# Second image's statistics by TensorE ones products, and a transposed embedding product, in a fused residual block

## The chip, the cores and the metric

The kernel runs on one core of one Trainium2 chip. The metric is the device time of one execution in microseconds (us); the runs of the kernel before gave 490.58, 489.97 and 493.06, a median of 490.58. Engines are named as in the profile: PE (TensorE matmul), PEld (its weight loads), DVE (VectorE), ACT (ScalarE), POOL (GpSimd), SP (SyncE, which issues most DMAs).

## The reference

```python
B, C, HW, E = 2, 512, 64, 1152
def reference(x, t_emb, g1, be1, w1, w_emb, g2, be2, w2):
    # gn: normalisation over 4 groups of 128 channels x 64 x 64; conv3: 3x3 convolution, 512 to 512 channels
    h = conv3(_silu(gn(x, g1, be1)), w1)
    emb = _silu(t_emb) @ w_emb
    h = h + emb.reshape(B, C, 1, 1)
    h = conv3(_silu(gn(h, g2, be2)), w2)
    return x + h
```

All inputs and the output are bfloat16. A group of the normalisation is exactly one tile of 128 channels, so its statistics are one mean and one variance per image and tile.

## The kernel before, in words

**Tiling.** The channels are four tiles (ct) of 128. The work is cut into eight chunks: layer 1 or 2, image 0 or 1, upper or lower half of the rows; chunks 0 and 1 are image 0 in layer 1, chunks 2 and 3 image 1 in layer 1, 4 to 7 the same in layer 2. A chunk has four units, one for each tile k of output channels. The convolution is a Winograd-like transform along the rows: the input side makes planes of the normalised rows (`rows_a`, `rows_b`: L614 to L663), PE multiplies them with transformed weights, ACT evacuates the PSUM banks with a scale (`evac_*`, L737 to L753), and DVE combines the results (L826 to L841).

**A unit** (`unit`, L713) in chunk 0 is a list of steps of 12 matmuls of 512 columns (4 tiles ct x 3 column taps): p2, p0, p1, p3 into rotating pairs of banks 0 to 5, p4 into bank 6 and p5 into bank 7. For the first three units p4 and p5 are made in the opening (L1091 to L1095), into banks 0 to 5, so banks 6 and 7 are first used for convolution in unit 3 of chunk 0. Chunks 1 to 3 have in place of p2 and p0 the steps B2, B0, A2, A0 of 256-column matmuls, with p4 in bank 6 ahead of B and p5 in bank 7 behind B.

**Statistics of image 1** (`stats1`, L1023). They are needed by the silu of chunk 2. `CFG["st1"]` (L205) says how each tile is summed. With 1 (tiles 0, 2, 3) ACT reads six pieces of 650 or 715 elements twice, once as Identity and once as Square, each with an accumulator output (L1031, L1032), and DVE adds the six partial sums (L1034 to L1038). With 0 (tile 1) DVE makes `bn_stats` of eight pieces (L1048) and `bn_aggr` (L1050). Tile k is registered behind unit k of chunk 0 (L1129). Then `gn_chain` (L429), put on the list `later` by tile 3 (L1056), sums over the 128 channels of a tile with `ones_neg` products into bank 7, copies the bank with DVE (L442) and makes scale and offset. It is registered behind the first unit of chunk 1.

**Embedding** (`emb`, L1058). Registered in chunk 0 ahead of unit 1. Three pieces of `w_emb` go through one buffer. Per piece three matmuls have `s_sb` (128 x 2, silu of `t_emb`) as weights and 512 columns of `w_emb` as moving data, into two partitions of bank 7. DVE copies them (L1071), and four fp32 transposes bring the 512 sums onto the 128 partitions, as `EMB`.

**Order of the work.** Each operation is registered with a planner (`Plan`, L26): engine, cost, read and written regions, from which follow its predecessors in the order of registration. Convolution steps are chained in the order of registration; other PE operations float. `solve` (L143) simulates the engines as in-order queues with these costs and `emit` (L164) writes the instructions in the order of the start times found. So who stands behind whom on an engine comes from the planner, while two operations on one PSUM bank keep their order of registration. All DMAs of the parts spoken of here are issued by SP, in that order.

Of the kernel before, what the change touches and what calls it, by code (L numbers as in the profile page):

```python
# [10 lines left out]
ACT = mybir.ActivationFunctionType  # L11
# [165 lines left out]
def _idx(off, dims):  # L177
# [7 lines left out]
RW = 65  # L185
# [19 lines left out]
    'st1': (1, 0, 1, 1),  # L205
# [9 lines left out]
def kernel(  # L215
# [807 lines left out]
    def stats1(ct):  # L1023
        nm = f"st1{ct}"
        me, mq = ME1 + ct, ME1 + CT + ct
        if CFG["st1"][ct]:
            part = Fc(12)
            for i, (ch, r0, n) in enumerate([(ch, r0, n) for ch in range(2) for r0, n in ((1, 11), (12, 11), (23, 10))]):
                d = A(VB[0] + (2 * (ct % 2) + i % 2) * VP + 3120, [[1, n * RW]], BF16)
                dma(d.ap, x[1, ct, ch][:, r0 * RW:(r0 + n) * RW], [], [d], P * n * RW * 2, nm)  # L1030
                act(A8(JNK, n * RW), d, ACT.Identity, acc=F(part + i), name=nm)  # L1031
                act(A8(JNK, n * RW), d, ACT.Square, scale=float(HW) ** -0.5, acc=F(part + 6 + i), name=nm)  # L1032
            wj = Fc(6)
            pl.op("DVE", 0.1, lambda: nc.vector.tensor_scalar(  # L1034
                out=F(wj, 6).ap, in0=F(part, 6).ap, scalar1=1.0 / HW, scalar2=0.0, op0=ALU.mult, op1=ALU.add,
                accum_out=F(me).ap), regs(F(part, 6)), regs(F(wj, 6), F(me)), nm)
            pl.op("DVE", 0.1, lambda: nc.vector.reduce_sum(out=F(mq).ap, in_=F(part + 6, 6).ap, axis=AX.X),  # L1037
                  regs(F(part + 6, 6)), regs(F(mq)), nm)  # L1038
        else:
            bst, mv = Fc(48), Fc(2)  # L1040
            for i in range(4):
                d = A(W2O[0], [[1, 16 * RW]], BF16)
                r0 = 1 + 16 * (i % 2)
                dma(d.ap, x[1, ct, i // 2][:, r0 * RW:(r0 + 16) * RW], [], [d], P * 32 * RW, nm)
                for h in range(2):
                    e = A(W2O[0] + h * 8 * RW, [[RW, 8], [33, 2], [1, 32]], BF16)
                    q = F(bst + 12 * i + 6 * h, 6)
                    pl.op("DVE", 0.61, lambda e=e, q=q: nc.vector.bn_stats(out=q.ap, in_=e.ap), regs(e), regs(q), nm)  # L1048
# [8 lines left out]

    def emb():  # L1058
        nm = "emb"
        pe = R(psum[0:BB, 7 * 512:8 * 512], ("P", np.array([7])), 512)  # L1060
        lst = []
        lds = []
        for i0, n in ((0, 3), (3, 3), (6, 3)):
# [142 lines left out]
```

## Time and profile before

| | |
|---|---|
| median of 3 runs | 490.58 us |
| the profiled execution: time, span | 490.7 us, 488.9 us |
| PE busy | 460.8 us (94%), 2853 matmuls |
| PE weight loads | 279.1 us (57%) |
| DVE busy | 435.8 us (89%) |
| ACT busy | 379.8 us (78%) |
| POOL busy | 37.4 us (8%) |
| DMA | 87.17 MB, mean 178 GB/s |

The profile is of one execution. In the waits view a row says which engine's line waited for which engine's line, the sum in us, how often and the longest. In the timeline a row is a run of equal instructions: start, duration, engine, line, operation, output and input with sizes, count, and in brackets the idle time ahead of it and what ended it. In the windows view a row is a stretch: its length, the busy time and count of PE, PEld, DVE, ACT and POOL, the clock granted to PE, and the DMA share with GB/s. A group row gives the total busy time and the mean duration in ns, then idle time ahead. L380 is the helper that issues all matmuls, L329 DVE's two-operand operations, L352 all ACT operations, L365 the DMAs. The ends of matmuls are modelled; their starts are not.

### The profile page before, as it was taken

The page shows a single profiled execution, that of the slowest core. Times are in us where ns is not written, and L with a number is a line of the kernel's source. Part 1 is how long each engine was busy: PE and PEld are TensorE (multiplying, and loading weights), DVE is VectorE, ACT ScalarE, POOL GpSimd, SP SyncE. Part 2 cuts the span into 40 slices and gives each one's busy share as a digit, 9 for nine tenths or more (in the row PEclk, how much of TensorE's full clock was granted, in tenths as well). Part 3 has the DMA queues.
Part 4 walks back from the last instruction along what each step waited for, and adds up shares of the span by engine and source line. Part 5 has one row for each costly group of instructions (what it writes and reads, how often), then busy time and mean ns, then how long its engine had stood idle before and what let it go on. Part 6 is the DMA issues. An engine that isn't in the chain of part 4 may idle for free. (4 is left out here: it accounts for less than half of the span.)

```text
span 488.9 us, 8107 instructions
## 1 busy us (share of the span) xinstructions
PE 460.8 (94%) x2853; PEld 279.1 (57%) x2853; DVE 435.8 (89%) x865; ACT 379.8 (78%) x612; POOL 37.4 (8%) x66
## 2 busy tenths in 40 slices
PE   6999999777499999999999998999999999999995
PEld 5744344343255555555555555666666667676783
DVE  1699999997869999998899999998799999998547
ACT  4887899999699987859997886865977579656552
POOL 3100000000100001010000000112111021001000
PEclk9999999989599999999999999999999999999999
DMA  8754463464832336657477776685956769737524
GB/s 329 296 168 116 154 182 117 155 200 135 287 105 108 114 114 181 177 152 278 137 280 266 278 260 211 146 211 135 242 149 183 196 175 248 172 82 139 122 45 87
DMA packets 41080, 87.17 MB, mean 178 GB/s; under 512 B 6480, under 2 KB 16720, under 8 KB 41040
## 3 DMA queue, kind: packets, MB, share of 16 engines
q1 hardware_dynamic: 36096, 77.60, 47.7%
q0 software_dynamic: 4656, 9.05, 12.4%
q8 instruction: 22, 0.36, 0.3%
q14 instruction: 18, 0.15, 0.1%
q10 hardware_dynamic: 288, 0.01, 0.0%
HBM read 62.25 MB, written 31.32 MB: 191 GB/s over the span
## 5 line engine op out<-in xcount | busy, mean ns | idle before, releaser
L380 PE MATMUL psum<-ar 128*128 128x256 f16 (+2 forms) x2737 | 445.5, 325 | 11.7 <-DVE ar L329 5.7
L329 DVE TENSOR_TENSOR ar<-ar 128x1040 f16<-128x1040 f16 (+6 forms) x689 | 405.8, 647 | 31.4 <-ACT ar L352 26.9
L380 PEld LDWEIGHTS <-ar 128*128 128x128 f16 (+1 forms) x2729 | 266.5, 99 | 187.6 <-issue 17.3
L352 ACT ACTIVATE ar<-ar 128x384 bf16<-128x384 bf16 (+6 forms) x205 | 169.1, 856 | 50.9 <-DVE ar L329 45.7
L352 ACT ACTIVATE ar<-psum 128x512 f16<-128x512 f32 (+2 forms) x220 | 152.5, 718 | 40.7 <-PE psum L380 31.3
L352 ACT ACTIVATE ar<-ar,fs 128x2112 f16<-128x2112 bf16 (+1 forms) x32 | 68.6, 2148 | 5.9 <-DMA ar<-h_scr 3.3
L333 DVE TENSOR_SCALAR ar<-ar 128x512 f16<-128x512 f16 (+2 forms) x73 | 26.2, 380 | 2.0 <-ACT ar L352 2.0
L365 POOL DMA_DIRECT2D out_dram<-ar x15 | 18.1, 1206 | 108.9 <-DVE ar L329 108.9
L352 ACT ACTIVATION_READ_ACCUMULATOR ar<-psum 128x1 f32 x96 | 19.7, 205 | 0.0
L451 POOL TENSOR_TENSOR fs<-fs 128x1 f32<-128x1 f32 (+1 forms) x7 | 7.6, 1083 | 137.4 <-DVE fs L449 137.4
L369 POOL MEMSET ar<- 128x65 f16 (+5 forms) x28 | 4.4, 197 | 123.6 <-DVE ar L329 47.2
L380 PE MATMUL psum<-ar,ones_bf 128*128 128x260 bf16 x64 | 9.6, 308 | 4.4 <-DMA ar<-in_x_dram 4.4
L380 PE MATMUL psum<-fs,ones_neg 128*128 128x1 f32 (+3 forms) x36 | 5.2, 258 | 7.0 <-DVE fs L1037 7.0
L352 ACT ACTIVATION_READ_ACCUMULATOR ar<-ar 128x1 f32 x56 | 11.1, 198 | 0.0
L380 PEld LDWEIGHTS <-ones_bf 128*128 128x128 bf16 x64 | 6.7, 108 | 6.2 <-issue 3.1
L380 PEld LDWEIGHTS psum<-fs,ones_neg 128*128 128x128 f32 x36 | 5.0, 206 | 8.1 <-DVE fs L1037 7.2
L365 POOL DMA_DIRECT2D ar<-ar x4 | 3.7, 931 | 71.3 <-DVE ar L329 60.5
L968 DVE SCALAR_TENSOR_TENSOR ar<-psum,ident 128x128 bf16<-128x128 f32 x4 | 1.2, 289 | 5.6 <-PE psum L380 5.6
L1048 DVE BATCH_NORM_STATS2 fs<-ar 128x6 f32<-128x512 bf16 x8 | 5.3, 680 | 0.0
L442 DVE COPY fs<-psum 128x2 f32<-128x2 f32 (+1 forms) x7 | 1.1, 159 | 4.4 <-PE psum L380 4.4
L453 DVE TENSOR_TENSOR fs<-fs 128x1 f32<-128x1 f32 (+1 forms) x7 | 1.1, 155 | 1.9 <-POOL fs L451 1.9
L411 ACT ACT_TABLE_LOAD x1 | 1.3, 1283 | 1.7 <-PEq L1190 1.7
(50 smaller groups left out, 23.1 us busy)
## 6 DMA issues: line engine op xcount, KB each, us to landing
ar<-in_w_dram SPq DMA_DIRECT2D x32, 384.0 KB, 4.0
ar<-in_x_dram SPq DMA_DIRECT2D x16, 552.5 KB, 4.0
h_scr<-ar SPq DMA_DIRECT2D x16, 520.0 KB, 3.1
ar<-h_scr SPq DMA_DIRECT2D x16, 520.0 KB, 3.5
out_dram<-in_x_dram SPq DMA_DIRECT2D x30, 260.0 KB, 4.2
out_dram<-ar POOLq DMA_DIRECT2D x15, 520.0 KB, 6.1
u_scr<-ar SPq DMA_DIRECT2D x16, 384.0 KB, 3.1
ar<-u_scr SPq DMA_DIRECT2D x4, 1536.0 KB, 7.4
```

The source lines that it names most:

```text
L329: pl.op("DVE", 0.075 + 0.000521 * out.n, lambda: nc.vector.tensor_tensor(out=out.ap, in0=a.ap, in1=b.ap, op=op), regs(a, b), regs(out), name)
L333: pl.op("DVE", cost or 0.075 + 0.00026 * out.n, lambda: nc.vector.tensor_scalar(out=out.ap, in0=a.ap, scalar1=s, scalar2=None, op0=ALU.mul ...
L352: lambda: nc.scalar.activation(out=out.ap, in_=a.ap, func=func, scale=sc, **kw), regs(*rr), regs(*ww), name)
L365: lambda: eng.dma_start(out=out, in_=in_, **kw), regs(*r), regs(*w), name, lat=3.2 if sw else None, after=after, sw=sw)
L369: pl.op("POOL" if eng == "gpsimd" else "DVE", 0.08 + 0.0005 * out.n, lambda: e.memset(out.ap, v), (), regs(out), name)
L380: nc.tensor.matmul(out.ap, lhsT=lhsT.ap, rhs=rhs.ap, start=st, stop=sp, skip_group_check=True)
L411: nc.scalar.activation(out=fs[:, WARM:WARM + 1], in_=fs[:, WARM + 1:WARM + 2], func=ACT.Silu)
L442: pl.op("DVE", 0.16, lambda: V.tensor_copy(out=F(tot, 2 * n).ap, in_=ps.ap), regs(ps), regs(F(tot, 2 * n)), name)
L451: pl.op("POOL", 0.85, lambda: nc.gpsimd.tensor_tensor(out=F(rs, n).ap, in0=N.ap, in1=F(NEGH, n).ap, op=ALU.pow), regs(N), regs(F(rs, n)), ...
L453: small(lambda: V.tensor_mul(out=S.ap, in0=F(rs, n).ap, in1=F(g, n).ap), [F(rs, n)], [S], name)
L968: pl.op("DVE", 0.3, lambda: nc.vector.scalar_tensor_tensor(out=j2.ap, in0=g.ap, scalar=1.0 / HW, in1=ident[:], op0=ALU.mult, op1=ALU.mult, ...
L1048: pl.op("DVE", 0.61, lambda e=e, q=q: nc.vector.bn_stats(out=q.ap, in_=e.ap), regs(e), regs(q), nm)
```

## The change

`stats1` has one form for all four tiles. A tile comes in four pieces of 1040 elements, in three slots that rotate (the free tails of three planes of chunk 0). Over each piece PE runs four products of 260 columns with a matrix of ones as weights (`cone`), all sixteen of a tile accumulated in bank 6 or 7 by turns; ACT squares the piece once, with an accumulator; at the end ACT sums the 260 columns of the bank with one Identity with accumulator. DVE adds four partial sums of squares. Identity passes over the data, `bn_stats` and the table `st1` are gone. The four tiles are registered ahead of chunk 0's units, and `gn_chain` right behind unit 3 of chunk 0, where it was behind the first unit of chunk 1. `emb` is registered ahead of these, with five loads of `w_emb` into places that are free in the opening, and 36 products with blocks of `w_emb` (128 x 128) as weights and `s_sb` (2 columns) as moving data; the sums land on the 128 partitions as `EMB` needs them, with no copy and no transposes.

```diff
-    'st1': (1, 0, 1, 1),
...
     def stats1(ct):
         nm = f"st1{ct}"
         me, mq = ME1 + ct, ME1 + CT + ct
-        if CFG["st1"][ct]:
-            part = Fc(12)
-            for i, (ch, r0, n) in enumerate([(ch, r0, n) for ch in range(2) for r0, n in ((1, 11), (12, 11), (23, 10))]):
-                d = A(VB[0] + (2 * (ct % 2) + i % 2) * VP + 3120, [[1, n * RW]], BF16)
-                dma(d.ap, x[1, ct, ch][:, r0 * RW:(r0 + n) * RW], [], [d], P * n * RW * 2, nm)
-                act(A8(JNK, n * RW), d, ACT.Identity, acc=F(part + i), name=nm)
-                act(A8(JNK, n * RW), d, ACT.Square, scale=float(HW) ** -0.5, acc=F(part + 6 + i), name=nm)
...
+        bk = 6 + ct % 2
+        part = Fc(4)
+        for i in range(4):
+            pb = VB[0] + (ct * 4 + i) % 3 * VP + 3120
+            d = A(pb, [[1, 1040]], BF16)
+            r0 = 1 + 16 * (i % 2)
+            dma(d.ap, x[1, ct, i // 2][:, r0 * RW:(r0 + 16) * RW], [], [d], P * 2080, nm)
+            mm([(Ps(bk, 0, [[1, 260]]), cone, A(pb + 260 * q, [[1, 260]], BF16),
+                 i == 0 and q == 0, i == 3 and q == 3) for q in range(4)], nm, chain=False)
+            act(A8(VB[0] + 3 * VP + 3120 + i % 2 * 520, 1040), d, ACT.Square, scale=float(HW) ** -0.5, acc=F(part + i), name=nm)
+        act(A(VB[0] + 3 * VP + 3120, [[1, 260]], BF16), Ps(bk, 0, [[1, 260]]), ACT.Identity, scale=1.0 / (P * HW), acc=F(me), name=nm)
+        pl.op("DVE", 0.1, lambda: nc.vector.reduce_sum(out=F(mq).ap, in_=F(part, 4).ap, axis=AX.X),
+              regs(F(part, 4)), regs(F(mq)), nm)
...
     def emb():
         nm = "emb"
-        pe = R(psum[0:BB, 7 * 512:8 * 512], ("P", np.array([7])), 512)
...
+        at = [VB[0] + i // 2 * VP + 3120 + i % 2 * 512 for i in range(8)] + [JNK]
+        for i in range(0, ET, 2):
+            n = min(2, ET - i)
+            d = A(at[i], [[1, n * 512]], BF16)
+            dma(d.ap, w_emb[:, i:i + n, :].rearrange("p e o -> p (e o)"), [], [d], P * n * 1024, nm)
+        lst = [(Ps(7, k * BB, [[1, BB]]), A(at[i] + k * 128, [[1, 128]], BF16), R(s_sb[:, i, :], K("s_sb"), 2),
+                i == 0 and k == 0, i == ET - 1 and k == CT - 1) for i in range(ET) for k in range(CT)]
         mm(lst, nm, chain=False)
...
     ucnt[0] = 0
+    emb()
+    for ct in range(CT):
+        stats1(ct)
...
-                if k == 1:
-                    emb()
...
             run_later = list(later)
-            later.clear()
+            if c == 0 and k < CT - 1:
+                run_later = []
+            for f in run_later:
+                later.remove(f)
             unit(c, k, opening=2 if c == 0 and k < 3 else 0)
             for f in run_later:
                 f()
-            if c == 0:
-                stats1(k)
```

The planner then finds another order on every engine. Three places follow; line numbers of the change are one less than those of before from L206 on.

On PE, before, the products of image 1's `gn_chain` (the two rows with `ones_neg`) stand between the last B step (128x256) and step p5 (128x8x2x32 and 128x512) of the second unit of chunk 1:

```order
L380 LDWEIGHTS ar
L380 MATMUL psum<-ar 128x256
L380 MATMUL psum<-fs,ones_neg 128x8 [waits DVE_49]
L380 MATMUL psum<-fs,ones_neg 128x4
L380 LDWEIGHTS ar
L380 MATMUL psum<-ar 128x8x2x32 [waits DVE_49]
```

In the change they stand inside the B steps of the first unit of chunk 1:

```order
L379 LDWEIGHTS ar
L379 MATMUL psum<-ar 128x256
L379 MATMUL psum<-fs,ones_neg 128x8 [waits Activation_49]
L379 MATMUL psum<-fs,ones_neg 128x4
L379 LDWEIGHTS ar
L379 MATMUL psum<-ar 128x256
```

So they moved ahead by about one unit of 80 matmuls, and what follows them directly is no longer a step that uses their bank.

On ACT, before, from unit 3 of chunk 0 on (128x512 from psum are evacuations, 128x8x2x32 those of p4 and then p5, 128x715 and 128x650 the pieces of image 1's tile 2, 128x384 the first weights of layer 2):

```order
L352 ACTIVATE ar,fs<-psum 128x512 [waits PE_49]
L352 ACTIVATE ar,fs<-ar 128x715 [waits Activation_49]
L352 ACTIVATE ar,fs<-psum 128x8x2x32 [waits DVE_49]
L352 ACTIVATE ar,fs<-ar 128x650 [waits DMAHW2_49,Activation_49]
L352 ACTIVATE ar<-ar 128x512 [waits DVE_49]
...
L352 ACTIVATE ar,fs<-ar 128x715 [waits Activation_49]
L352 ACTIVATE ar,fs<-psum 128x8x2x32 [waits DVE_49]
L352 ACTIVATE ar,fs<-ar 128x715 [waits DMAHW5_49,Activation_49]
L352 ACTIVATE ar<-ar 128x384 [waits DMAHW4_49]
```

In the change, from the last pieces of tile 3 (128x1040) on, with the last evacuation of the sums (128x260):

```order
L351 ACTIVATE ar,fs<-psum 128x8x2x32 [waits PE_49]
L351 ACTIVATE ar,fs<-ar 128x1040 [waits DMAHW3_49,Activation_49]
L351 ACTIVATE ar<-ar 128x512
L351 ACTIVATE ar,fs<-psum 128x512 x2
L351 ACTIVATE ar,fs<-ar 128x2080 [waits Pool_49]
L351 ACTIVATE ar,fs<-psum 128x260 [waits PE_49,Activation_49]
L351 ACTIVATE ar<-ar 128x384 [waits DMAHW4_49]
L351 ACTIVATE ar<-ar 128x384 [waits DMAHW5_49]
L351 ACTIVATE ar<-ar 128x512 [waits DVE_49]
L351 ACTIVATE ar,fs<-psum 128x8x2x32 [waits PE_49]
```

All pieces of image 1 now stand ahead of the evacuation of p5 of unit 3; before, those of tile 3 and a third of those of tile 2 stood behind it. The 128x2080 is the square of a unit's result, which now stands between the last piece and the last sum.

On PE in the change, the last groups of ones products stand inside step p0 of unit 3, each group behind its load (DMAHW):

```order
L379 LDWEIGHTS ones_bf
L379 MATMUL psum<-ar,ones_bf 128x260 [waits DMAHW2_49]
L379 LDWEIGHTS ones_bf
...
L379 MATMUL psum<-ar,ones_bf 128x260 [waits DMAHW3_49]
...
L379 LDWEIGHTS ar [waits DVE_49]
...
L379 MATMUL psum<-ar 128x8x2x32 [waits Activation_49]
```

The last row is the first matmul of p5 of unit 3, six matmuls of p0 behind the last group. Before, no ones products stood in the units. The 36 products of the embedding stand in the opening, among its p4 and p5 products; before, three groups of three stood in units 0 to 2, and the transposes behind them.

38 lines of the change are left out of this document (removed).

## The prediction

> **What bounds the kernel now.** First I read the slices of the page, then the waits of the two stretches in which TensorE (PE) is not full, then the timeline there.
>
> ```profile
> PE   6999999777499999999999998999999999999995
> PEclk9999999989599999999999999999999999999999
> ```
>
> A slice is 12.2 us. PE is full but for the opening, slices 7 to 10 (86 to 134 us) and the tail, and the granted clock drops in slices 8 and 10. From 134 us to 473 us PE's work is an all but unbroken stream, so a microsecond taken out ahead of it moves the end by about one, as long as VectorE (DVE) and ScalarE (ACT) can follow. The waits of 80 to 110 us and of 110 to 145 us, the rows of PE:
>
> ```profile
> PE psum L380 <- DVE ar L329: 3.8, 2, 3.5
> PE psum L380 <- ACT ar L352: 2.2, 1, 2.2
> ...
> PE psum L380 <- DVE fs L1037: 7.0, 1, 7.0
> PE psum L380 <- DVE fs L442: 2.2, 1, 2.2
> ```
>
> The four long ones sum to 2.2 + 3.5 + 7.0 + 2.2 = 14.9 us. What is behind the 7.0 and the second 2.2 stands in the timeline:
>
> ```profile
> 123.19 0.20 ACT L352 ACTIVATION_READ_ACCUMULATOR ar<-ar 128x1 f32 x1
> ...
> 125.97 0.15 DVE L1037 TENSOR_REDUCE fs<-fs 128x1 f32<-128x6 f32 x1
> ...
> 126.19 1.01 PE L380 MATMUL psum<-fs,ones_neg 128*128 128x8 f32 x4 [6.95 <-DVE fs L1037]
> ...
> 129.41 15.76 PE L380 MATMUL psum<-ar 128*128 128x512 f16 x80 [2.21 <-DVE fs L442]
> ```
>
> The `ones_neg` products are those of the second image's `gn_chain`. They use PSUM bank 7, and so does step p5 of unit 1 of chunk 1 behind them; in PE's queue nothing passes them. So PE stands until the last squares of that image have left ACT (123.4), DVE has summed them (126.1) and copied the bank (129.4). ACT is late because it is full:
>
> ```profile
> 60.00:80.00 20.00, 20.00 (x94) 8.95 (x93) 19.22 (x39) 19.50 (x47) 0.00 (x0) 1.00 0.55 159
> 101.70:105.10 3.40, 3.40 (x18) 2.24 (x16) 3.40 (x9) 2.75 (x9) 0.00 (x0) 0.50 0.72 258
> 129.40:132.40 3.00, 2.99 (x8) 1.05 (x8) 2.88 (x8) 0.52 (x1) 0.93 (x1) 0.50 0.81 262
> ```
>
> Columns: stretch, length, busy PE, weight loads, DVE, ACT, POOL, granted clock, DMA. From 60 to 80 us ACT is busy 19.5 of 20. After each of the two groups of waits PE works at half clock, for 3.4 us and for 3.0 us.
>
> **The change, part by part.** The sum is made against the profiled execution's 490.7 us (span 488.9, 1.8 around it); the runs' median is 490.58, the same within 0.1, so nothing is converted.
>
> *ACT and DVE.* The rows of the three tiles that went through ACT and the one that went through DVE:
>
> ```profile
> L352 ACT ACTIVATE ar<-ar 128x715 fp8e4<-128x715 bf16 x24 | 19.1, 797 | 0.2 <-DMA ar<-in_x_dram 0.2
> L352 ACT ACTIVATE ar<-ar 128x650 fp8e4<-128x650 bf16 x12 | 8.9, 745 | 0.3 <-DMA ar<-in_x_dram 0.3
> L1048 DVE BATCH_NORM_STATS2 fs<-ar 128x6 f32<-128x512 bf16 x8 | 5.3, 680 | 0.0
> ```
>
> The accumulator read that follows each overlaps it in part, so the pair takes from ACT what lies between its start and that of the next instruction:
>
> ```profile
> 87.21 1.94 ACT L352 ACTIVATE ar<-ar 128x2080 fp8e4<-128x2080 f16 x1 [0.19 <-DVE ar L329]
> ...
> 89.14 0.58 ACT L352 ACTIVATE ar<-psum 128x512 f16<-128x512 f32 x1
> ...
> 89.71 0.79 ACT L352 ACTIVATE ar<-ar 128x715 fp8e4<-128x715 bf16 x1
> ...
> 90.49 0.58 ACT L352 ACTIVATE ar<-psum 128x512 f16<-128x512 f32 x1
> ```
>
> 0.78 us for 715 elements, 1.93 for 2080. Out go 24 x 0.78 + 12 x about 0.73 = 27.5 us. In come 16 squares of 1040 (between the two rows, 1.05 each: 16.8) and four evacuations of 260 columns (from 0.58 for 512, at most 0.5 each: 2.0), 18.8. ACT saves 8.7 us before the sums are needed. DVE loses 5.3 us of statistics, the embedding's 512-wide copy and some ten operations on a few columns, by estimate 6.5 in all. Both lie beside PE, so neither is a term. They decide whether the waits go. Where the sums are done and needed in the new order, on the clock of before:
>
> ```profile
> 99.60 0.59 ACT L352 ACTIVATE ar<-psum 128x512 f16<-128x512 f32 x1
> ...
> 100.82 18.41 PE L380 MATMUL psum<-ar 128*128 128x512 f16 x99 [3.46 <-DVE ar L329]
> ```
>
> The first row is the evacuation of p5 of unit 3; in the order of the change the last evacuation of the sums stands on ACT ahead of it, so 24 us ahead of 123.4. The second row is PE in p4 of the first unit of chunk 1; the `gn_chain` products now stand among the B steps right behind it, later than the sums. I take all four waits as gone: **-14.9**. Two of them (3.5 and the first 2.2) are of other work: chunk 1's planes from DVE, and the evacuation of bank 6 by ACT behind the squares. With DVE 6.5 and ACT 8.7 us lighter and PE arriving later, both should be on time. If these two stay, 5.7 less is saved. PE's ends are modelled, with a mean of 388 ns for a matmul that follows its predecessor by about 223:
>
> ```profile
> L380 PE MATMUL psum<-ar 128*128 128x512 f16 x1248 | 290.3, 388 | 11.1 <-DVE ar L329 5.3 <-DVE fs L442 3.4 <-ACT ar L352 2.2
> ```
>
> so each wait hides up to 0.17 more; three of the four follow such a matmul: **-0.5**. The half clock goes with the waits: (3.4 + 3.0) / 2 = **-3.2** (0 if waits over some 3 us remain).
>
> *The ones products.* 64 of 260 columns, each with its weight load, enter PE's stream where it is full. The opening of before has the same instruction in a stream:
>
> ```profile
> 18.46 1.98 PE L380 MATMUL psum<-ar,ones_bf 128*128 128x260 bf16 x16
> 20.27 1.24 PE L380 MATMUL psum<-ar 128*128 128x128 bf16 x17
> 21.44 0.83 PE L380 MATMUL psum<-fs,ones_neg 128*128 128x2 f32 x6
> ```
>
> Sixteen from 18.46 to 20.27 are 0.113 each: **+7.2**. Nothing hides them. The rows of the weight loads, of 128 columns, of the ones and of the embedding's 2 columns:
>
> ```profile
> L380 PEld LDWEIGHTS <-ar 128*128 128x128 f16 x1888 | 184.9, 98 | 87.9 <-issue 2.4 <-DVE ar L329 0.8
> L380 PEld LDWEIGHTS <-ones_bf 128*128 128x128 bf16 x64 | 6.7, 108 | 6.2 <-issue 3.1 <-DVE ones_bf L386 1.2
> L380 PEld LDWEIGHTS <-s_sb 128*2 128x2 bf16 x9 | 0.5, 82 | 1.7 <-issue 1.3
> ```
>
> With loads of 108 ns that no longer overlap it would be 14: the upper bound. Below 7 there is no reason to go.
>
> *The embedding product.* Out of the units go nine products, three at a time, and the transposes behind them:
>
> ```profile
> 51.49 0.81 PE L380 MATMUL psum<-ar,s_sb 128*2 128x512 bf16 x3
> 52.24 6.85 PE L380 MATMUL psum<-ar 128*128 128x512 f16 x30
> ...
> L380 PE MATMUL psum<-ar 2*128 2x2 f32 x8 | 1.0, 249 | 0.0
> ```
>
> 3 x 0.75 + at most 1.0 = -3.2. Into the opening come 36 pairs of a 128-column load and a 2-column product. The nearest row is the 17 products of 128 columns above, from 20.27 to 21.44: 0.069 a pair, +2.5; 0.1 a pair (a bare load) would make 3.6. They stand among the opening products, where PE waits a little anyway:
>
> ```profile
> 32.45 19.11 PE L380 MATMUL psum<-ar 128*128 128x512 f16 x84 [0.67 <-DVE ar L329]
> ```
>
> That covers 0.7 of it. Net -3.2 + 2.5 - 0.7 = **-1.4** (0 to -2). [...] The five loads of `w_emb` are queued on SyncE behind most of the first weights, ahead of the last four 192 KB weight loads; the DMA engines have room for them in the ten us behind:
>
> ```profile
> 20.00:30.00 10.00, 10.00 (x70) 6.24 (x69) 8.44 (x25) 9.08 (x13) 1.74 (x2) 1.00 0.15 56
> ```
>
> The share of 0.15 (56 GB/s) leaves the 1.2 MB time before PE is at the last two channel tiles. If those weights came late, the opening products of these tiles would wait.
>
> *What is late next.* The new sums sit in banks 6 and 7. Unit 3's p4 and p5 use those banks, so p5 must wait for the evacuation of the last sum. Six matmuls (1.3 us) lie between the last ones product and p5; the evacuation takes 0.6 and may stand behind a 2080-wide square of 1.93. That is 0 to 3.0 (square, evacuation, and a product late by a landing); I take 1.93 + 0.6 - 1.3 = **+1.2**. Behind p5 in PE's queue stand p1 and p3 of the unit, and ACT's evacuations wait for them.
>
> Sum: -14.9 - 0.5 - 3.2 + 7.2 - 1.4 + 1.2 = -11.6, **479.1 us**.
>
> **The rivals.**
>
> *DVE becomes the bound.* For: it is nearly full behind the stall, and PE would run 12 us ahead of where DVE stood.
>
> ```profile
> 102.00:112.00 10.00, 10.00 (x55) 5.85 (x54) 8.93 (x27) 9.35 (x24) 0.00 (x0) 0.84 0.63 213
> 112.00:122.00 10.00, 7.23 (x41) 3.80 (x39) 7.68 (x16) 9.21 (x24) 0.00 (x0) 1.00 0.45 120
> ...
> 132.00:142.00 10.00, 10.00 (x54) 5.18 (x53) 4.61 (x10) 8.29 (x11) 0.73 (x1) 0.98 0.39 135
> ...
> 160.00:170.00 10.00, 10.00 (x55) 5.19 (x53) 9.90 (x21) 9.94 (x17) 0.00 (x0) 1.00 0.28 87
> ```
>
> Against: in the first three rows it idles 1.1 + 2.3 + 5.4 = 8.8 us, because the second image's planes could not be made without its sums; that idle time and the 6.5 of removed work make 15.3, more than PE's 11.6. If it cannot use the idle time, the end moves by the 6.5 alone: 484.2.
>
> *The banks and loads take back a part.* p4 and p5 of unit 3 wait the full 3.0 each, and the 3.5 for chunk 1's planes stays: -11.6 + 4.8 + 3.5 = -3.3, 487.4. For: ACT and DVE are full up to there. Against: both have less to do.
>
> *Slower: PE stands for its loads.* Each ones group is in PE's queue and waits for its piece; each piece needs one of three slots, which is free again only when PE and ACT have both read it, and its load is issued by SyncE in order, behind loads that wait for other buffers.
>
> ```profile
> ar<-in_x_dram SPq DMA_DIRECT2D x4, 260.0 KB, 2.8
> ...
> DMA to landing us min/median/max: 2.3/3.9/8.2
> ```
>
> A turn of a slot is a landing, the wait in ACT's queue (some 2 us, an estimate) and the square: 2.8 + 2 + 1.05 = 5.9 us; 16 pieces over 3 slots are 5.3 turns, 31 us. From the first unit to p5 of unit 3, where all sums must be done, PE has 180 matmuls of 0.223 and the products: 40 + 7 = 47 us. So loads would have to be slow: with landings of 8.2 and 3 us in ACT's queue a turn is 12.3 and all are 65. PE stands 18 us, the 11.6 are gained, and half clock comes back for some 4 us (+2): 490.7 - 11.6 + 18 + 2 = 499. The point from which the kernel is slower is a turn of 10.7 us. [...] Against this rival: 179 KB pieces made ACT wait 0.5 us in all before, and the embedding's loads, in the same queue, made PE wait for nothing.
>
> *It does not do what it says:* the sums come no sooner, because a load or SyncE holds them. Then the 7.2 of products fall into PE's standing time ahead of the `gn_chain` products, and what is left is the embedding's -1.4: 489.3. Against it is the order: the last evacuation stands 24 us ahead.
>
> **How the numbers follow.** Forecast 0.68 (own range 476 to 483.5), DVE bound 0.12, banks and loads 0.09, slower 0.07, no effect 0.04. The range: below, the forecast without its 1.2 and without the waits of the 512-column row above that lie behind the four (5.3 - 3.8 and 3.4 - 2.2, 2.7 in all), 475.2, rounded to 475.5; above, the DVE rival with 2 us more, 486.0; about 0.18 lies outside. A measurement of this kernel can tell 1% (4.9 us) from no change. Faster by over 1% (under 485.7): 0.68 and most of the DVE rival, 0.80. Within 1%: the bank rival, the rival without effect and the rest, 0.13. Slower: 0.07.
>
> **What would show it.** Right: no PE wait over 2 us between 40 and 140 us; the `ones_neg` products of the second image before 110 us; 64 ones products among units 0 to 3 at 0.11 us each; ACT under 95% from 60 to 80 us; DVE at most 3 us idle from 100 to 140; the clock at 1.00 in the slices 8 to 10. Wrong: waits of PE for `in_x_dram` in the units (the slower rival), DVE rows ahead of PE's waits from 140 us on (the DVE rival), or PE waiting on ACT before p4 or p5 of unit 3 for over 3 us.

## The result and the profile after

The change takes **476.49 us** (476.18 to 478.71), before took 490.28 beside it: a ratio of 0.9716, 95% interval 0.9670 to 0.9762, so 2.8% faster. The profiled execution took 476.65 us with a span of 474.9 (before 490.7 and 488.9): 14.05 less, where 11.6 were predicted.

The slices of the page, PE's busy tenths and the clock:

```profile
PE   6998999899999999999999999999999999999995
PEclk9998999999999999999999999999999999999999
```

The hole in slices 7 to 10 is filled but for one wait (the 8 of slice 7), and the clock is full there; one slice of the opening (35.6 to 47.5 us) has a lower clock, which no term of the prediction had. The waits view from 80 to 145 us, PE's rows, where before had 14.9 us in four, and from 145 to 400 us:

```profile
PE psum L379 <- ACT ar L351: 1.7, 1, 1.7
```

```profile
PE psum L379 <- DVE fs L441: 1.2, 2, 0.9
```

For the second stretch before had three rows:

```profile
PE psum L380 <- DVE ar L329: 1.3, 2, 0.9
PE psum L380 <- DVE fs L442: 1.2, 1, 1.2
PE psum L380 <- ACT ar L352: 0.3, 1, 0.3
```

What is left of PE's waits between 80 and 145 us is one, in PE's timeline at the end of p0 of unit 3 of chunk 0:

```profile
87.75 1.06 PE L379 MATMUL psum<-ar,ones_bf 128*128 128x260 bf16 x8
88.65 1.50 PE L379 MATMUL psum<-ar 128*128 128x512 f16 x6
91.86 0.83 PE L379 MATMUL psum<-ar 128*128 128x512 f16 x3 [1.72 <-ACT ar L351]
```

and on ACT at the same time:

```profile
89.40 1.95 ACT L351 ACTIVATE ar<-ar 128x2080 fp8e4<-128x2080 f16 x1
91.23 0.21 ACT L351 ACTIVATION_READ_ACCUMULATOR ar<-ar 128x1 f32 x1
91.32 0.40 ACT L351 ACTIVATE ar<-psum 128x260 bf16<-128x260 f32 x1
```

The last ones products end at 88.65, the six products of p0 fill PE until about 90.1, and p5 stands until ACT has done the 2080-wide square and then the evacuation of the last sum. Behind it the `gn_chain` products of image 1 now cost nothing:

```profile
99.65 4.37 PE L379 MATMUL psum<-ar 128*128 128x512 f16 x25
103.85 0.51 PE L379 MATMUL psum<-fs,ones_neg 128*128 128x8 f32 x4
104.22 28.05 PE L379 MATMUL psum<-ar 128*128 128x256 f16 x154
```

The ones products of the units (shortest, median and longest record in ns, first and last start in us) and the group row of the squares:

```profile
L379 PE MATMUL psum<-ar,ones_bf x64: 271/275/278, 50.1 to 88.5; 128*128 128x260 bf16 x64
```

```profile
L351 ACT ACTIVATE ar<-ar 128x1040 fp8e4<-128x1040 bf16 x16 | 17.0, 1062 | 0.6 <-ACT ar L351 0.2 <-DVE ar L328 0.2
```

Where in the program the time came from is seen by counting the products of each engine's order along the trace. Start of a step's first product, us, in the profiled executions of before, of the change, and of the change run a second time (further down):

| step | before | change | change again |
|---|---|---|---|
| unit 0 of chunk 0 | 40.7 | 42.8 | 42.0 |
| unit 3, p4 | 76.4 | 80.6 | 79.9 |
| unit 3, p5 | 84.9 | 91.9 | 91.4 |
| chunk 1, unit 0 | 95.2 | 99.9 | 99.4 |
| chunk 1, unit 1 | 114.7 | 114.6 | 113.9 |
| chunk 1, unit 2 | 140.6 | 128.8 | 128.1 |
| chunk 3, unit 0 | 227.1 | 215.2 | 214.9 |
| chunk 7, unit 0 | 434.4 | 420.7 | 420.4 |

Up to unit 0 of chunk 1 the change is 4.7 us behind; two units later it is 11.8 ahead, and 2 more come in small pieces later. The change again has the same order of instructions on every engine.

### The profile page after: what moved, and what is told of

Its sections match the earlier page's. It is cut to its first block, busy times and chain, and to the rows that moved or that the text cites. A ratio compares the mean times of both kernels' runs of the same rounds, so it can differ in the third digit from the quotient of the medians.

```text
span 474.9 us, 8229 instructions
## 1 busy us (share of the span) xinstructions
PE 461.3 (97%) x2936; PEld 283.4 (60%) x2936; DVE 428.2 (90%) x847; ACT 371.9 (78%) x580; POOL 38.8 (8%) x66
## 4 chain that ended last, share of the span: by engine, by line
PE 40%; DVE 24%; ACT 7%; issue 4%; POOL 0%; DVEq 0%; ACTq 0%; POOLq 0%
PE psum L379 40%; DVE ar L328 22%; ACT ar L351 7%; DVE ar L332 2%; POOL fs L450 0%; POOL ar L364 0%; DVEq L1176 0%; DVE fs L441 0%; DVE fs L914 0%; DVE fs L915 0%; DVE fs L452 0%; DVE fs L917 0%; DVE fs L921 0%; DVEq L328 0%; ACTq L351 0%
## 5 line engine op out<-in xcount | busy, mean ns | idle before, releaser
L379 PE MATMUL psum<-ar 128*128 128x512 f16 (+2 forms) x2729 | 443.7, 325 | 4.3 <-ACT ar L351 1.7
L328 DVE TENSOR_TENSOR ar<-ar 128x1024 f16<-128x1024 f16 (+5 forms) x689 | 404.0, 648 | 27.4 <-ACT ar L351 24.2
L351 ACT ACTIVATE ar<-psum 128x512 f16<-128x512 f32 (+2 forms) x224 | 156.5, 714 | 53.3 <-PE psum L379 44.7
L351 ACT ACTIVATE ar<-ar 128x512 f16<-128x512 f16 (+6 forms) x185 | 158.1, 890 | 31.2 <-DVE ar L328 30.2
L364 POOL DMA_DIRECT2D out_dram<-ar x15 | 18.1, 1207 | 115.9 <-DVE ar L328 91.8
L379 PE MATMUL psum<-ar,ones_bf 128*128 128x260 bf16 x128 | 18.3, 284 | 4.5 <-DMA ar<-in_x_dram 4.5
L351 ACT ACTIVATION_READ_ACCUMULATOR ar<-psum 128x1 f32 x100 | 20.8, 208 | 0.0
L379 PEld LDWEIGHTS <-ones_bf 128*128 128x128 bf16 x128 | 12.6, 100 | 9.9 <-issue 3.2
L450 POOL TENSOR_TENSOR fs<-fs 128x1 f32<-128x1 f32 (+1 forms) x7 | 9.0, 1281 | 108.9 <-DVE fs L448 97.2
L351 ACT ACTIVATION_READ_ACCUMULATOR ar<-ar 128x1 f32 x36 | 7.1, 198 | 0.0
```

Of the source, the lines that this page charges most:

```text
L328: pl.op("DVE", 0.075 + 0.000521 * out.n, lambda: nc.vector.tensor_tensor(out=out.ap, in0=a.ap, in1=b.ap, op=op), regs(a, b), regs(out), name)
L351: lambda: nc.scalar.activation(out=out.ap, in_=a.ap, func=func, scale=sc, **kw), regs(*rr), regs(*ww), name)
L364: lambda: eng.dma_start(out=out, in_=in_, **kw), regs(*r), regs(*w), name, lat=3.2 if sw else None, after=after, sw=sw)
L379: nc.tensor.matmul(out.ap, lhsT=lhsT.ap, rhs=rhs.ap, start=st, stop=sp, skip_group_check=True)
L450: pl.op("POOL", 0.85, lambda: nc.gpsimd.tensor_tensor(out=F(rs, n).ap, in0=N.ap, in1=F(NEGH, n).ap, op=ALU.pow), regs(N), regs(F(rs, n)), ...
```

## The experiments

The times are medians of four to ten executions; before stood at 490.2 to 490.5 beside each group. The expectations of some runs count the images from one: their "image 2" is the second image, image 1 of the text above.

**1. The order alone.** Before, with `gn_chain` registered behind unit 1 of chunk 1.

```diff
-            later.clear()
+            if c == 1 and k == 0:
+                run_later = []
+            for f in run_later:
+                later.remove(f)
```

> The kernel before, with one edit: the second image's gn_chain is registered behind unit 1 of chunk 1 instead of behind unit 0, so that p5 of unit 1 no longer stands behind it in bank 7. The sums are still made by ACT and DVE as before. Theory (late sums): the 7.0 and 2.2 us waits on PE go from that place, but chunk 2's planes cannot be made without the sums, which still come at about 123 us, so DVE stands and PE waits at the first unit of chunk 2 or at p4 and p5 of unit 2 for some 6 to 9 us: 484 to 489 us. Rival (order alone): the whole loss came from where the products stood in the queue; 490.3 - 9.2 - 1.5 = 480 or less, with no new wait.

485.81 us, ratio 0.9904 (0.9876 to 0.9931). It leaves out one dependency: tile 0 of chunk 2 is registered ahead of `gn_chain`, so its silu does not wait for the statistics and works with a scale and offset that are not made yet. Chunk 1 gains all that the change gains (its unit 2 starts at 126.1, before at 140.6), and then, as the theory said, PE stands at the first unit of chunk 2 for DVE's planes:

```profile
152.79 3.50 PE L380 MATMUL psum<-ar 128*128 128x512 f16 x15
156.79 0.83 PE L380 MATMUL psum<-ar 128*128 128x512 f16 x3 [0.49 <-DVE ar L329]
166.55 3.78 PE L380 MATMUL psum<-ar 128*128 128x512 f16 x14 [8.94 <-DVE ar L329]
```

**2. The order alone, with the dependency.** Tile 0 of chunk 2 is registered behind `gn_chain` as well.

```diff
...
+            if c == 1 and k == 1:
+                prod(2, 0)
-            if c + 1 < 8:
+            if c + 1 < 8 and not (c == 1 and k == 0):
                 prod(c + 1, k)
```

> The kernel before, with image 2's statistics chain asked for behind unit 1 of chunk 1 and the first tile of image 2's chunk asked for behind it in turn, so that nothing stands ahead of what it needs. Theory (the place of the chain alone cannot bring the gain, since sums that end late push the first tile of image 2 late): waits at chunk 1 shrink as in the earlier run of this kind, and a wait for VectorE of 7 to 12 us stands at the first unit of chunk 2; 484 to 491. Rival (order alone is the gain): 480 or less.

492.67 us, ratio 1.0036 (1.0016 to 1.0055), 1.7 above the theory's range and far from the rival's. PE, at the same place:

```profile
157.63 2.83 PE L380 MATMUL psum<-ar 128*128 128x512 f16 x12
165.01 1.44 PE L380 MATMUL psum<-ar 128*128 128x512 f16 x3 [4.55 <-DVE ar L329]
173.46 2.93 PE L380 MATMUL psum<-ar 128*128 128x512 f16 x10 [7.00 <-DVE ar L329]
```

Unit 2 of chunk 1 starts at 130.3, 10 us ahead of before; unit 1 of chunk 2 at 187.0, 3 behind it. The stall is only pushed from the users of bank 7 to the users of the statistics. For the 7.0 and the second 2.2 us of before the late sums were the cause, not the place of the chain.

**3. The change without ones products.** The sums by Identity passes on ACT over the same 1040-wide pieces, whose four results DVE adds; all else as in the change.

```diff
...
-            mm([(Ps(bk, 0, [[1, 260]]), cone, A(pb + 260 * q, [[1, 260]], BF16),
-                 i == 0 and q == 0, i == 3 and q == 3) for q in range(4)], nm, chain=False)
+            act(A8(VB[0] + 3 * VP + 3120 + i % 2 * 520, 1040), d, ACT.Identity, scale=1.0 / HW, acc=F(part + 4 + i), name=nm)
...
```

> The change without the ones products: each piece of 1040 elements is read twice by ACT, as Identity and as Square, each with accumulator; pieces, slots and the place of registration are those of the change. PE has 7.2 us less, ACT some 15 us more than in the change. Theory (ACT was the late engine): ACT is full again ahead of chunk 1, PE waits for evacuations in units 2 and 3 and for the first planes of chunk 2: 478 to 484 us, with PE waits on ACT of 6 us or more between 60 and 170 us. Rival (larger pieces and the earlier registration were enough, the products only cost): 476.5 - 7.2 - 1.7 = 468 to 471 us.

485.04 us, ratio 0.9894 (0.9862 to 0.9926), 1.0 above the theory's range; the profiled execution took 482.04. PE is rid of 7.2 us of products, and waits instead, for ACT in unit 3 and at the start of chunk 1 (98.53):

```profile
81.63 3.06 PE L379 MATMUL psum<-ar 128*128 128x512 f16 x13
88.97 4.46 PE L379 MATMUL psum<-ar 128*128 128x512 f16 x12 [4.28 <-ACT ar L351]
94.65 2.83 PE L379 MATMUL psum<-ar 128*128 128x512 f16 x12 [1.21 <-ACT ar L351]
98.53 1.72 PE L379 MATMUL psum<-ar 128*128 128x512 f16 x7 [1.06 <-ACT ar L351]
```

and 3.4 us for DVE at the first unit of chunk 2. So of the 13.8 us, the ones products bring 8.6 by the medians (485.04 - 476.49 = 8.55) and 5.4 between the profiled executions (482.04 - 476.65): 7.2 us on the fullest engine are the cheaper price. The profiled execution lies 3.0 us under the median of its run, and its mean granted clock is 0.995 where the other three have 0.985 to 0.988; so up to 3 of the 8.6 us may be clock that this trace does not show.

**4. The embedding alone.** Before, with the change's embedding in the opening and nothing else.

```diff
...
+    emb()
     for c in range(8):
...
-                if k == 1:
-                    emb()
```

> The kernel before, with the transposed embedding product in the opening alone; the second image's sums as before. Theory: the 7.0 us wait of PE on the last sums stays, as ACT is as full as it was; 3.2 us go out of the units and 1.0 us and a half clock come into the opening: 488 to 491 us. Rival (embedding is a main part): 484 us or less.

491.89 us, ratio 1.0030 (1.0012 to 1.0047), 0.9 above the theory's range. The units run 3.6 us earlier by p4 of unit 3 (72.8 against 76.4), then PE waits for DVE, whose transformed weights are late (the weight loads stand 8.2 us for DVE between 78 and 92 us), and 7.29 us at `gn_chain` as before:

```profile
80.27 1.46 PE L380 MATMUL psum<-ar 128*128 128x512 f16 x3 [3.33 <-DVE ar L329]
85.24 6.96 PE L380 MATMUL psum<-ar 128*128 128x512 f16 x21 [3.51 <-DVE ar L329]
```

Alone it is worth nothing: PE comes 3.6 us sooner to waits that end when they ended.

**5. The change with the embedding's old form** at the new place.

```diff
...
-        lst = [(Ps(7, k * BB, [[1, BB]]), A(at[i] + k * 128, [[1, 128]], BF16), R(s_sb[:, i, :], K("s_sb"), 2),
...
+            lst = [(pe, R(s_sb[:, i0 + i, :], K("s_sb"), 2), A(W2O[1] + i * 512, [[1, 512]], BF16),
+                    i0 + i == 0, i0 + i == ET - 1) for i in range(n)]
...
```

> The change, with the embedding product in its old form (s_sb as weights, 512 moving columns, one buffer, copy and transposes), registered where the new one is. Theory (the form is worth little on PE): the old form puts 3.2 us of PE work and a wait for its loads into the first units where the new one put 1.0 us and a half clock of 1.7 us into the opening: 477 to 480 us, and no half clock at 38 us. Rival (the transposed form is a main part of the gain): 482 us or more.

482.07 us, ratio 0.9828 (0.9804 to 0.9851), in the rival's range, though its reason cannot be read off this run. The planner made another opening of it, with a half clock of its own from 42.2 to 45.6 us where none was expected (the 30 products from 41.34 take 8.47 us, 30 from 50.48 take 6.85); PE there:

```profile
36.21 1.50 PE L379 MATMUL psum<-ar,ones_bf 128*128 128x260 bf16 x12
37.64 0.81 PE L379 MATMUL psum<-ar,s_sb 128*2 128x512 bf16 x3
41.34 6.91 PE L379 MATMUL psum<-ar 128*128 128x512 f16 x23 [2.88 <-DVE ar L328]
```

Unit 0 starts at 47.0 (+4.2), p4 of unit 3 at 87.9 (+7.3, of which about 3 are the old form's own products), and two of the 7.3 come back later. How much the form alone is worth stays open.

**6. The embedding's pairs spread**, six behind each group of opening products of tile 3, with the loads issued beside that tile's.

```diff
...
+            if ct == CT - 1:
+                emb_part(12 * j, 12 * j + 6)
...
+            if ct == CT - 1:
+                emb_part(12 * j + 6, 12 * j + 12)
...
```

> The change, with the 36 pairs of the embedding no longer in one run between the opening's last product and unit 0, but six behind each of the six groups of products of the opening's tile 3; its loads are issued with tile 3's. Question: where the half clock of 3.4 us at the start of unit 0 (37.8 to 41.3 us in the change, about 1.7 us of lost time) comes from. Theory A: from the run of 36 two-column products, which count for little to whatever sets the clock. Then with the pairs spread there is full clock from unit 0 on, unit 0's p4 of unit 3 comes 1 to 2 us earlier than the change's 80.6, and the time is 474.5 to 475.8. Theory B: from the wait of 1.3 us for DVE ahead of unit 0 alone. Then the half clock stays, and the time is 476 to 477.5. Rival on cost: if the pairs cost 0.069 each when they don't run together, the opening grows by 1.5 us and the time is 477 to 478.5.

476.40 us, ratio 0.9719 (0.9705 to 0.9734). The clock stays full, as A said (the granted clock of the profiled execution is 0.998 on average, the change's 0.996), and unit 0 starts at 41.3; p4 of unit 3 comes only 0.6 us earlier (80.0), and the time does not follow. PE, in unit 3:

```profile
80.03 0.83 PE L379 MATMUL psum<-ar 128*128 128x512 f16 x3 [1.20 <-ACT ar L351]
91.81 12.15 PE L379 MATMUL psum<-ar 128*128 128x512 f16 x60 [1.82 <-ACT ar L351]
```

Most of the 1.5 us that PE was earlier is a wait for ACT at p4 of unit 3, and p5 starts at 91.8 or 91.9 in both. Among other products six pairs take 0.16 us, 0.027 each. A's time, and B's half clock, both missed.

**7. The change again**, to see whether the half clock belongs to it.

> The change once more, for the clock at the start of unit 0. If the half clock of 3.4 us (37.8 to 41.3 us) belongs to the change (the run of 36 small products and the wait behind it), the profile shows it again and unit 0 starts at 42.8. If it is an accident of the one execution, as its absence in the two runs that kept the run of 36 products suggests, unit 0 starts at 40.5 to 41.5 and the profile shows instead a wait for ScalarE of 1 to 2 us ahead of p4 of unit 3; either way 476.0 to 476.9, since p4 of unit 3 starts at 80 to 81 us in both.

475.96 us, ratio 0.9698 (0.9671 to 0.9724). PE in the opening:

```profile
35.69 1.04 PE L379 MATMUL psum<-s_sb,ar 128*128 128x2 bf16 x36
38.00 6.17 PE L379 MATMUL psum<-ar 128*128 128x512 f16 x27 [1.26 <-DVE ar L328]
```

The same order, the same 36 pairs and the same wait of 1.26, at full clock: the half clock does not follow from the order alone, so its absence in run 6 need not come from the spreading. What differs between the two executions is set out at the end. Unit 0 starts at 42.0, between the two cases that were expected; the wait ahead of p4 of unit 3 that the second case had does not come, since PE is there at 79.9, just when ACT is.

**8. Twice the ones products**, and half the scale in the pass that reads their sums.

```diff
-                 i == 0 and q == 0, i == 3 and q == 3) for q in range(4)], nm, chain=False)
+                 i == 0 and q == 0 and r == 0, i == 3 and q == 3 and r == 1) for q in range(4) for r in range(2)], nm, chain=False)
...
```

> The change, with every ones product of image 2's sums issued twice (128 in place of 64) and the scale of the pass that reads the sum halved: 64 products of 260 columns more on TensorE, nothing else. Theory (TensorE sets the end of the whole stretch, so that the ones products stand in the sum at their full price): +64 x 0.113 = +7.2, so 483.0 to 484.5, and p4 of the first unit of chunk 1's second tile pair of products (unit 2 of chunk 1) starts at 135 to 137 instead of 128.8. Rival (ACT, which is 96% busy from 60 to 80 us in the change, or the loads set the pace there and part of the ones products is hidden): less than +4, so under 480.5.

482.69 us, ratio 0.9845 (0.9829 to 0.9862): 6.2 above the change, 6.7 above its second run, 0.3 below the theory's range; unit 2 of chunk 1 starts at 135.0. The planner moved the embedding's pairs forward (to 31.2), but unit 0 starts at 41.9, as in the second run. PE at p5 of unit 3:

```profile
94.29 1.05 PE L379 MATMUL psum<-ar,ones_bf 128*128 128x260 bf16 x8
95.18 1.50 PE L379 MATMUL psum<-ar 128*128 128x512 f16 x6
97.04 1.72 PE L379 MATMUL psum<-ar 128*128 128x512 f16 x7 [0.36 <-ACT ar L351]
```

Against the second run, 1.6 of the 7.2 us disappear in the wait for ACT (1.96 to 0.36), and chunk 1 starts 5.6 later (105.0 against 99.4). A new wait of 1.05 us stands behind it, for DVE at the copy of `gn_chain`'s bank (111.04), so unit 2 of chunk 1 is 6.9 later. So about three quarters of the price go through; that the time comes out near the theory's is in part this other wait.

**9. p5 behind p1 and p3** in chunk 0. The edit speaks of units 1 to 3, but only unit 3 has its p5 there; those of units 1 and 2 are made in the opening.

```diff
+            if u:
+                run([(p2, 1, plain_mms), (p2 + 1, 3, plain_mms)])
...
-            if u:
-                run([(p2, 1, plain_mms), (p2 + 1, 3, plain_mms)])
```

> The change, with the products p5 of image 1's conv units behind p1 and p3 in units 1 to 3, not ahead of them, so that p5 of unit 3 no longer stands right behind the evacuation of image 2's last sum. Theory (the wait of 1.72 us at p5 of unit 3 is a wait for bank and evacuation alone, and the work behind it can fill it): the wait is gone, 1.3 to 1.9 us less, 474.5 to 475.5. Rival (ACT is the late engine there whatever the order, the wait only moves to p1 or p3 or to the first product of chunk 1): 476 to 478.

476.64 us, ratio 0.9724 (0.9709 to 0.9738): the rival. The wait moved, to p4 and to the later p5:

```profile
80.45 6.17 PE L379 MATMUL psum<-ar 128*128 128x512 f16 x27 [1.63 <-ACT ar L351]
96.64 6.81 PE L379 MATMUL psum<-ar 128*128 128x512 f16 x36 [0.88 <-ACT ar L351]
```

**10. The same, and the second GroupNorm's statistics later** in chunks 2 and 4.

```diff
-            if c == 0 and k < CT - 1:
+            if c == 0 and k < CT - 1 or c in (2, 4) and k == 0:
```

> The run before, and in chunks 2 and 4 the statistics of the second GroupNorm registered one unit later, so that they don't stand in bank 7 and on DVE at the place where the change's trace shows TensorE waiting 1.03 us (176 us) and 0.49 us (289 us). Theory: these waits go as well, 1.0 to 1.5 us less than the run before it, 473.0 to 474.5. Rival (DVE, 90% busy, gives the wait back at the next unit): within 0.5 us of the run before it.

475.75 us, ratio 0.9708 (0.9694 to 0.9723): 0.9 less than run 9, between theory and rival, and above the times that the theory gave. Of the two waits behind 145 us one is gone, the other became 1.14 us at 191.2. It is the lowest of these orders, but its interval overlaps that of the change's second run (0.9671 to 0.9724); a version that clearly beats the change was not found.

**11. Half the squares left out**: every second piece of the second image is not squared, so its second moment comes from half of the points.

```diff
-            act(A8(VB[0] + 3 * VP + 3120 + i % 2 * 520, 1040), d, ACT.Square, scale=float(HW) ** -0.5, acc=F(part + i), name=nm)
+            if i % 2 == 0:
+                act(A8(VB[0] + 3 * VP + 3120 + i % 2 * 520, 1040), d, ACT.Square, scale=float(HW / 2) ** -0.5, acc=F(part + i // 2), name=nm)
...
```

> The change, with half of the squares of image 2 left out: ScalarE squares every second piece of 1040 (8 of 16 passes, 8 x 1.06 = 8.5 us of ScalarE less), and the scale is doubled, so the second moment of image 2 is taken from half of its points; TensorE's work is the same. Theory (through 60 to 92 us ScalarE and TensorE are both full, and ScalarE holds TensorE at p5 of unit 3, 1.72 us, or, where TensorE comes out of the opening earlier, at p4 of unit 3 as well): these waits go, the time is 473.5 to 475.5. Rival (the waits are of one place and give way to a wait for VectorE, 90% busy): 476 to 477.5.

478.10 us, ratio 0.9734 (0.9711 to 0.9758), above both expectations. The planner, with fewer operations, wrote another opening, and unit 0 starts at 44.8, behind a wait of 1.91 and a half clock of its own (0.50 from 39.66 to 43.07):

```profile
39.16 13.14 PE L379 MATMUL psum<-ar 128*128 128x512 f16 x51 [1.91 <-DVE ar L328]
84.13 6.17 PE L379 MATMUL psum<-ar 128*128 128x512 f16 x27 [1.32 <-ACT ar L351]
```

The wait at p5 is gone, yet one of 1.32 for ACT stands at p4, and unit 0 is 2.0 us later than in the change, 2.8 later than in its second run. So this run does not answer the question; the next one keeps the order.

**12. Short squares, order kept**: each square reads 260 of its 1040 elements, the planner counts 1040. The second moment comes from a quarter of the points.

```diff
...
-            act(A8(VB[0] + 3 * VP + 3120 + i % 2 * 520, 1040), d, ACT.Square, scale=float(HW) ** -0.5, acc=F(part + i), name=nm)
+            sq(A8(VB[0] + 3 * VP + 3120 + i % 2 * 520, 1040), d, A8(VB[0] + 3 * VP + 3120 + i % 2 * 520, 260),
+               A(pb, [[1, 260]], BF16), F(part + i), nm)
```

> The change, with every square of image 2 taken over 260 of its 1040 elements (the scale is raised to match, so the second moment comes from a quarter of the points), while the planner still counts the full length: every engine's order is that of the change, only ScalarE's 16 passes become shorter, by about 0.6 us each (9 to 10 us in all). Theory (ScalarE holds TensorE at p5 of unit 3, and nothing else stands behind that): the wait of 1.7 to 2.0 us there goes, unit 0 of chunk 1 starts at 97.2 to 98.2 in place of 99.4 to 99.9, and the time is 473.8 to 475.0. Rival (VectorE, 90% busy, holds the place at once): p5 of unit 3 or the first steps of chunk 1 wait for VectorE instead, and the time is 475.5 to 476.9.

475.42 us, ratio 0.9704 (0.9682 to 0.9725); the profiled execution, 474.63, is 1.7 under that of the change's second run. The squares take 412 ns in place of 1062, and PE's waits from 85 to 170 us are:

```profile
88.97 12.15 PE L379 MATMUL psum<-ar 128*128 128x512 f16 x60 [0.23 <-ACT ar L351]
102.82 70.37 PE L379 MATMUL psum<-ar 128*128 128x512 f16 x394 [0.90 <-DVE fs L441]
```

Both theories have a part. ACT lets go (1.96 to 0.23; chunk 1 starts at 97.0), and 0.90 of it is given back 14 us later, where DVE is late with the copy of `gn_chain`'s bank. The median lies between the two ranges, and its interval overlaps that of the change's second run, so the time does not decide it; the trace shows both waits, and unit 2 of chunk 1 1.4 us earlier (126.7 against 128.1), of which 0.6 come from the opening.

## Why the prediction was right

**The four waits, -14.9: right.** None is left, and the two of other work (3.5 for planes, 2.2 for bank 6) went too, as forecast. For the 7.0 and the second 2.2 the cause, late sums, is shown by runs 1 to 3: the new place of the chain alone gives +0.4%, and with the sums still on ACT only about a third of the gain comes. For the other two it is argued, by ACT and DVE being lighter; run 3, with ACT loaded again, has ACT's part back (4.28, 1.21 and 1.06 us) and no wait for chunk 1's planes.

**The half clock, -3.2: right** in the slices 8 to 10. The new half clock in the opening (3.4 us) goes with 0.7 us more at unit 2 of chunk 1 (128.8 against 128.1 of the second run) and 0.3 at chunk 7.

**The ones products, +7.2: right.** A group of four starts 0.45 us ahead of what follows (87.75 to 88.65 for eight), 16 x 0.45 = 7.2. "Nothing hides them" is a little too strong: doubled, 5.6 of the second 7.2 us reach chunk 1, and the rest goes into the wait for ACT (run 8).

**p5 of unit 3, +1.2: right in its mechanism**, square, evacuation and six products of cover as worked out; 1.72 and 1.96 measured, inside 0 to 3.0. What the sum had at nothing is that ACT comes to the square 0.75 us behind the last ones product (89.40 against 88.65); the evacuation was shorter than put, 0.40 for 0.6. Its reading as a matter of one place was too narrow: runs 6 and 9 show the wait at p4 as soon as PE is earlier. ACT is late for PE at both places.

**ACT under 95% from 60 to 80 us: wrong.** It was busy 19.29 of 20, 96%:

```profile
60.00:80.00 20.00, 20.00 (x108) 10.22 (x106) 18.84 (x41) 19.29 (x41) 0.00 (x0) 1.00 0.63 193
```

The step said that ACT "saves 8.7 us before the sums are needed". Over the whole execution it nearly does (busy 379.8 us before, 371.9 after, 7.9 less), but all four tiles now stand ahead of p5 of unit 3, where before those of tile 3 and part of tile 2 stood behind. In the windows from 42 to 92 us, before and after:

```profile
42.00:92.00 50.00, 49.71 (x225) 21.24 (x224) 49.15 (x101) 44.33 (x95) 0.00 (x0) 1.00 0.47 145
```

```profile
42.00:92.00 50.00, 48.28 (x250) 24.15 (x248) 47.88 (x103) 48.16 (x107) 0.00 (x0) 1.00 0.53 159
```

ACT has 3.8 us more to do there, not less. It costs only the 1.7 at p5, since PE has 7.2 more to do as well.

**The embedding, -1.4: two sizes off.** The 36 pairs were priced at 0.069 each, 2.5; they start every 0.025 us from 34.82 to 35.70, and with the length of the last, 0.16, that is 1.0. The 0.7 of wait that was to cover them did not: a wait of 1.26 stands behind them. Unit 0 starts 2.1 us later, part of it the half clock there, and 1.3 later in the second run at full clock, where 1.8 was predicted; that the two errors all but cancel is luck. Out of the units came some 3.8 for the 3.2: from unit 0 to p4 of unit 3 before took 35.7, the change 37.8 with 52 ones products, 5.9, among them. And the term is not a gain of its own (run 4): it counts only because the waits behind it are gone.

**DVE as the bound: not seen, but near.** The windows from 100 to 140 us have 0.9 us of DVE idle, under the 3 that were given; rows:

```profile
100.00:110.00 10.00, 9.96 (x65) 6.11 (x63) 9.33 (x23) 9.98 (x25) 1.31 (x1) 1.00 0.63 204
110.00:120.00 10.00, 10.00 (x55) 5.21 (x54) 9.91 (x22) 10.00 (x17) 0.00 (x0) 1.00 0.62 220
120.00:130.00 10.00, 10.00 (x55) 5.20 (x54) 9.97 (x20) 9.81 (x16) 0.00 (x0) 1.00 0.32 108
130.00:140.00 10.00, 10.00 (x63) 5.96 (x61) 9.93 (x22) 10.00 (x17) 0.00 (x0) 1.00 0.43 132
```

It used the idle time that the prediction gave it, and hardly more was there; its work fell by 7.6 (435.8 to 428.2 us busy) for the estimated 6.5. PE's two waits behind 145 us do stand for DVE, the sign that was named for this rival, but they are 1.2 us in all where before had 2.5 of DVE. The slower rival fell: PE waited for no `in_x_dram` load in the units.

**Where the missing 2.45 us are.** From unit 0 of chunk 0 to unit 2 of chunk 1 the terms give -14.9 - 0.5 - 3.2 + 7.2 - 3.2 + 1.2 = -13.4; measured 99.9 - 86.0, -13.9. The opening gave +2.1 for +1.8. The rest, -2.2, lies behind unit 2 of chunk 1: before waited 0.92, 1.23, 0.36 and 0.28 us there, the change 0.86 and 0.32, and by the prediction's estimate (388 - 223 ns) each wait takes up to 0.17 more than its row. The prediction knew these waits (2.7 us "behind the four") but used them for the range's low end only, and put them at nothing in the sum. Its 2.7 was misread besides: the 512-column row counts the whole execution, and 0.67 (at 32.45 us) and 0.29 (at 81.51) of it lie ahead of the four. That the waits shrink because DVE and ACT have a lead is argued, not shown, and no run measures the -0.5 for modelled ends by itself.

## What to carry to other kernels

Work off a late engine can be worth more than it costs on the fullest one: 7.2 us on PE bought 8.6 us net here by the medians, 5.4 between the profiled executions, because what was late stood in front of PE; count when the last sum is ready, not how busy an engine is on average. When work moves ahead of a deadline, add up what each engine has to do ahead of that deadline, before and after: here ACT's busy time fell by 7.9 us in all and rose by 3.8 in the windows ahead of the deadline. In a kernel whose order a planner makes, test a cost by shortening an operation with its planned cost kept, since otherwise the new order answers for you.

## What the runs showed of the hardware

**Half clock in steps of 3.41 us.** In the trace of the change the granted clock is 0.50 from 37.84 to 41.25 us, in that of before from 101.71 to 105.13 and from 122.19 to 132.43. That is 3.41, 3.41 and 10.24 us, three times 3.41; the second stretch of before starts 20.48 us behind its first, six times 3.41. Counted from the first record of the clock (7.11 us in the change, 9.55 in before), the changes of the clock in these two traces all lie a whole number of such steps later (in the change 9 and 10 of them, and 137 for the one in the tail). The step that lost it in the change and the next, and in the second run the step with the pairs, the one with the wait and the next, from the windows (span, PE busy, ..., granted clock):

```profile
34.42:37.84 3.42, 2.16 (x43) 1.47 (x42) 3.39 (x8) 3.42 (x2) 0.00 (x0) 1.00 0.07 17
37.84:41.25 3.41, 3.41 (x10) 1.20 (x9) 3.41 (x10) 2.21 (x7) 0.00 (x0) 0.50 0.79 216
```

```profile
33.14:36.55 3.41, 3.41 (x48) 1.93 (x46) 3.38 (x7) 3.41 (x4) 0.00 (x0) 1.00 0.00 0
36.55:39.97 3.42, 2.16 (x17) 1.00 (x14) 3.42 (x9) 3.42 (x5) 0.00 (x0) 1.00 0.38 98
39.97:43.38 3.41, 3.41 (x17) 1.51 (x16) 3.41 (x10) 3.41 (x11) 0.00 (x0) 1.00 0.79 243
```

With the same busy time, 2.16, the step of the change is followed by half clock and that of the second run is not. In the first, 1.0 us of it are the two-column pairs, and full-width products fill about a third of the step; in the second all pairs but one start in the step before, and full-width products fill 1.97 us. In run 12, with the change's order on PE, the step falls between these two cases:

```profile
35.35:38.77 3.42, 2.16 (x38) 1.34 (x35) 3.39 (x8) 3.42 (x4) 0.00 (x0) 1.00 0.27 48
38.77:42.18 3.41, 3.41 (x17) 1.50 (x16) 3.41 (x10) 3.41 (x13) 0.00 (x0) 1.00 0.80 259
```

What differs is the number of moving columns in the products that start in the step: 36 x 2 + 5 x 512 = 2632 in the change, 24 x 2 + 7 x 512 = 3632 in run 12, 2 + 9 x 512 = 4610 in the second run; unit 0 of the change, from 41.25, has 7680 in a step. In the traces of before and of the change half clock follows the steps with the fewest: 2304 (before, from 98.30), 512 (before, from 118.78), 2632, and the last step of each, with none. The fewest that kept it are 3072 (before, from 91.47) and 3584 (change, from 89.03). Busy time does not sort them: 2.16 us lost it in the change, and 1.56 and 1.70 us kept it in these last two. So in these traces the columns go with the clock; that they are its cause, and where a limit would lie, was not shown. The prediction tied the half clock to waits over some 3 us; in the step of the change the wait was 1.26, beside 1.0 of narrow products.

**Narrow pairs are cheap.** A 128-column weight load and a 2-column product take 0.025 us per pair in a run (36 start from 34.82 to 35.70), though each load's record is 96 ns long and each product's 163. By the prediction's 0.1 for a bare load, near the length of a load's record, 36 would take 3.6 us; the trace has 1.0. In run 6, in groups of six among other products, a pair takes 0.027.
